# One program order from a list scheduler, and FFN gradients turned from SBUF to SBUF, in a transformer block's forward and backward pass

## The chip, the cores and the metric

The kernel runs on one core of one Trainium2 chip. The metric is the device time of one execution in microseconds (us). The engines of the core are TensorE (PE in the profile, with its weight loads as PEld), VectorE (DVE), ScalarE (ACT), GpSimd (POOL) and SyncE (SP, which here only issues DMAs). Each engine works through its own instructions in order, and semaphores hold it until what it needs is there.

## The reference

Inputs are bf16: x is 2048 x 512, the attention has 32 heads of 16, the FFN has 1792 hidden units. The forward pass is

```
h  = x + A(layernorm(x))        # A: q, k, v = x @ wqkv; each position attends to
                                # itself and 7 earlier ones, 2 apart; then @ wo
h2 = h + B(layernorm(h))        # B: gelu(x @ w1 + b1) @ w2 + b2, gelu in the tanh form
```

The kernel returns h2 and, for a given gradient of h2, the gradients of x, wqkv, wo, w1, b1, w2 and b2. So it computes the forward pass, the backward pass through FFN, attention and both layernorms, and four large weight gradients, each a sum over all 2048 positions.

## The kernel before

The 2048 positions are cut into 4 chunks of 512 (`c`), each of 4 tiles of 128 rows. The work has three stages.

**Attention forward** (`p1_*`). For each chunk: layernorm (L192), turning by PE transposes (`to_fm`), q, k and v (L351), dots of q with 8 shifted copies of k (L258: one DVE multiplication of 128 x 4096, summed by PE), softmax, products of the coefficients with rows of v that are gathered from DRAM by an indirect DMA from POOL (L250; products L288, two per tile of 128 x 2048; PE sums them, L293), the output projection (L446), and a second layernorm.

**FFN, forward and backward** (`p2_h`, `p2_rest`). PE computes the hidden layer (L520); ACT evicts it twice, as x (L522) and as its square (L523); ten steps on blocks of 4 hidden tiles give the gelu and its derivative: 9 on DVE (L528 to L537) and a tanh on ACT (L530). PE then multiplies by w2 (L555; the bias b2 and the residual h are added by two more matmuls, L556 and L557), computes the gradient of the hidden layer (L568, multiplied by the derivative on DVE at L571) and takes it back through w1 (L581). The gelu (`g_d`) and the gradient (`gh_d`) are stored to DRAM as they lie, hidden units on partitions (L538, L574).

**Attention backward and weight gradients** (from L601). DVE carries the dots (L882) and the products with gathered rows (L787); PE sums them (L888, L795) and computes the gradients of q, k, v (L822, L850). The order here is written out by hand: `slot` advances delayed steps and gives PE a quota of weight-gradient matmuls, which the generator `wgrads` hands out one by one (L643). A weight gradient needs its operands with positions on partitions, so `load_t` (L636) loads g and gh back from DRAM with a transposing DMA, 256 hidden units at a time (1 MiB), into two buffers `gwm`. Loads of the q, k, v gradients (L697) and the rows of the first layernorm (L692, 32 small DMAs) come behind gates at the end.

Plain DMAs go out on SP or POOL; the indirect ones on POOL only. Stores of weight gradients (L629), of h2 (L560) and of the gradient of x (L856) are on POOL. Buffers are pools that are released between the stages (L496, L604). The key lines:

```
638  SY.dma_start_transpose(out=t_[:], in_=src)     # load_t: DRAM to SBUF, turned
655  tiles.append(load_t(g_d[n * 256:(n + 1) * 256, :] if n < 7 else gh_d[...]))
692  SY.dma_start(out=r16[32 * j:32 * j + 32, 2 * sc:2 * sc + 2, :], in_=ap)
754  filler(dve_us * RATIO - pe)                     # PE's quota of weight gradients
```

Of the kernel before, what the change touches and what calls it, by code (L numbers as in the profile page):

```python
# [1 line left out]

# [8 lines left out]
P = 128  # L11
# [13 lines left out]
NEG = -30000.0  # L25

# [5 lines left out]
def _sub(apobj, dims, off=0):  # L32
    return _ap(apobj, [apobj.ap[0]] + [list(d) for d in dims], off)


@with_exitstack
def kernel(
# [36 lines left out]
    FB = [(0, 4), (4, 8), (8, 12), (12, 14)]  # L74

    def pool(name, bufs=1, side="left", space=None):
        kw = dict(name=name, bufs=bufs, side=side)
        if space is not None:
            kw = dict(name=name, bufs=bufs, space=space)
        if space is not bass.MemoryType.DRAM:  # L80
            kw["reuse_waits"] = "tile"
        return tc.alloc_tile_pool(**kw)

    pools = []

    def LP(name, side="left"):
        p = pool(name, 1, side)
        pools.append(p)
        return p

    const = LP("const")
    dram = pool("dram", 1, space=bass.MemoryType.DRAM)
    psY = pool("psY", 2, space=bass.MemoryType.PSUM)
    psT = pool("psT", 2, space=bass.MemoryType.PSUM)
    psX = pool("psX", 2, space=bass.MemoryType.PSUM)

    def X(name):
        return psX.tile([P, 2, 512], F32, name=name, tag="x")

    def Y(name):  # L100
        return psY.tile([P, 512], F32, name=name, tag="y")

    def TT(name):
        return psT.tile([P, 1024], BF16, name=name, tag="t")


    ident = const.tile([P, P], BF16, name="ident")
    make_identity(nc, ident[:])
    Pmat = const.tile([P, P], BF16, name="Pmat")
    V.tensor_copy(out=_sub(Pmat[:], [[1, 8], [8, DH]]), in_=_sub(ident[:], [[DH, 8], [1, DH]]))  # L110
    S32 = const.tile([P, 32], BF16, name="S32")
    for j in range(4):
        V.tensor_copy(out=S32[32 * j:32 * j + 32, :], in_=ident[32 * j:32 * j + 32, 32 * j:32 * j + 32])
    Sum4 = const.tile([P, P], BF16, name="Sum4")
    V.tensor_copy(out=Sum4[:].rearrange("p (a b) -> p a b", a=4), in_=S32[:].unsqueeze(1).to_broadcast([P, 4, 32]))
    nSum4 = const.tile([P, P], BF16, name="nSum4")
    V.tensor_scalar(out=nSum4[:], in0=Sum4[:], scalar1=-1.0, scalar2=None, op0=ALU.mult)
    Sm = const.tile([P, 4, P], BF16, name="Sm")
# [10 lines left out]
    mk = const.tile([16, 2, 4, 32], BF16, name="mk")  # L129
# [52 lines left out]

    def to_fm(src, dst):
        for hh in range(2):
            pt = TT("pt")
            for d2 in range(2):
                dc = 2 * hh + d2
                for j in range(TPC):
                    T.transpose(pt[:, d2 * 512 + j * P:d2 * 512 + (j + 1) * P], src[:, j, dc * P:(dc + 1) * P], ident[:])
            A.copy(out=dst[:, 2 * hh:2 * hh + 2, :], in_=pt[:].rearrange("p (a n) -> p a n", a=2))  # L190

    def layernorm(wp, src, rstd_all, c, dst):  # L192
        mv = wp.tile([P, TPC, 2], F32, name="mv", tag="mv", bufs=2)
        for j in range(TPC):
# [830 lines left out]
```

## Time and profile before

| | us |
|---|---|
| timed runs | 896.83, 905.11, 908.13 (median 905.11) |
| profiled execution: span from first to last instruction | 887.3 |
| PE busy, matmuls | 665.3 (75% of the span) |
| DVE busy | 530.4 (60%) |
| ACT busy | 339.6 (38%) |
| POOL busy | 175.3 (20%) |

The profile has no time of the profiled execution outside its span; the timed runs are 9.5 to 20.8 us longer than that span (the median 17.8 us). A busy share is a mean over stages with different limits, so the windows of the trace by stage are read first: 0 to 154 us is attention forward, 154 to 234 the passage to the FFN, 234 to 432 the FFN, 432 to 740 attention backward with weight gradients beside it, 740 to the end weight gradients alone. The granted TensorE clock is given as a share of full speed.

### The profile page before, as it was taken

The page shows a single profiled execution, that of the slowest core. Times are in us where ns is not written, and L with a number is a line of the kernel's source. Part 1 is how long each engine was busy: PE and PEld are TensorE (multiplying, and loading weights), DVE is VectorE, ACT ScalarE, POOL GpSimd, SP SyncE. Part 2 cuts the span into 40 slices and gives each one's busy share as a digit, 9 for nine tenths or more (in the row PEclk, how much of TensorE's full clock was granted, in tenths as well). Part 3 has the DMA queues.
Part 4 walks back from the last instruction along what each step waited for, and adds up shares of the span by engine and source line. Part 5 has one row for each costly group of instructions (what it writes and reads, how often), then busy time and mean ns, then how long its engine had stood idle before and what let it go on. Part 6 is the DMA issues. An engine that isn't in the chain of part 4 may idle for free.

```text
span 887.3 us, 10335 instructions
## 1 busy us (share of the span) xinstructions
PE 665.3 (75%) x3948; PEld 302.2 (34%) x3948; DVE 530.4 (60%) x774; ACT 339.6 (38%) x529; POOL 175.3 (20%) x221
## 2 busy tenths in 40 slices
PE   4888886467889899899853779791777688864486
PEld 2434432222334333334321324240222356731132
DVE  6799696368768687694657967972494852000000
ACT  2657674366445356340430533440233331100011
POOL 3304342200100001000006431240143222210011
PEclk9999997778999999999965789896787898977699
DMA  9637276841232233233994587899589654632343
GB/s 304 201 142 261 90 236 223 183 127 62 71 119 91 88 96 106 72 118 120 281 264 148 195 261 237 243 273 83 74 256 346 217 160 113 149 110 77 137 146 116
DMA packets 151280, 146.30 MB, mean 165 GB/s; under 512 B 94669, under 2 KB 139518, under 8 KB 146366
## 3 DMA queue, kind: packets, MB, share of 16 engines
q1 hardware_dynamic: 137102, 74.83, 33.5%
q0 software_dynamic: 14128, 70.81, 23.2%
q8 instruction: 31, 0.51, 0.2%
q14 instruction: 19, 0.16, 0.1%
HBM read 72.95 MB, written 48.03 MB: 136 GB/s over the span
## 4 chain that ended last, share of the span: by engine, by line
issue 30%; PE 13%; DVE 11%; DMA 7%; POOL 6%; ACT 3%; SPq 0%; POOLq 0%; DVEq 0%; ACTq 0%
DMA R<-q_d,rowi 4%; POOL out_dram L629 3%; PE ps_f L555 3%; DVE prb L787 2%; DMA R<-go_d,rowi 2%; PE ps_gg L568 2%; PE ps_gw L651 2%; PE ps_gl L581 2%; PE ps_h L520 1%; POOL R L250 1%; PE ps_go L822 1%; POOL out_dram L856 1%; DVE junk L219 1%; DVE gt L532 1%; ACT xb L522 1%
## 5 line engine op out<-in xcount | busy, mean ns | idle before, releaser
L787 DVE TENSOR_TENSOR prb<-R,cf 128x2048 bf16<-128x2048 bf16 x96 | 110.4, 1217 | 22.6 <-DMA R<-q_d,rowi 14.6
L520 PE MATMUL ps_h<-ln2T,w 128*128 128x512 bf16 x224 | 63.4, 411 | 23.3 <-ACT x L523 20.7
L651 PE MATMUL ps_gw<-gout_r,gwm 128*128 128x512 bf16 x224 | 61.0, 413 | 25.0 <-DMA gwm<-g_d 25.0
L795 PE MATMUL ps_band<-prb,S 128*32 128x512 bf16 x384 | 41.4, 466 | 44.6 <-DVE prb L787 43.7
L709 PE MATMUL ps_gwq<-gqh,ln_r 128*128 128x512 bf16 x192 | 44.0, 390 | 30.7 <-DMA gqh<-gq_d 25.9
L568 PE MATMUL ps_gg<-goT,w2T 128*128 128x512 bf16 x224 | 54.5, 378 | 11.0 <-DVE gb1p L571 8.6
L672 PE MATMUL ps_gw<-gwm,ln_r 128*128 128x256 bf16 x448 | 55.4, 282 | 8.3 <-ACT gwst L628 8.2
L629 POOL DMA_DIRECT2D out_dram<-gwst x58 | 31.4, 542 | 148.0 <-ACT gwst L628 107.3
L211 ACT ACTIVATE gyr<-ps_gl,rstd 128x512 bf16<-128x512 f32 x32 | 21.9, 686 | 99.0 <-PE ps_gl L850 65.3
L522 ACT ACTIVATE xb<-ps_h,b1c 128x512 bf16<-128x512 f32 x56 | 38.2, 686 | 45.0 <-PE ps_h L520 44.8
L555 PE MATMUL ps_f<-w,gt 128*128 128x512 bf16 x224 | 54.1, 384 | 1.0 <-DVE gt L532 1.0
L560 POOL DMA_DIRECT2D out_dram<-h2s x16 | 9.4, 591 | 227.9 <-ACT h2s L559 227.9
L351 PE MATMUL ps_qkv<-ln1T,wqkv 128*128 128x512 bf16 x192 | 49.3, 397 | 6.4 <-ACT kt L353 2.1
L672 PEld LDWEIGHTS <-ln_r 128*128 128x128 bf16 x448 | 44.5, 101 | 19.2 <-issue 12.5
L850 PE MATMUL ps_gl<-wqkvT,gqkvT 128*128 128x512 bf16 x192 | 46.1, 398 | 0.0
L219 DVE CUSTOM_DVE_ANT_0 junk<-gyr,ln1r 128x512 bf16<-128x512 bf16 x16 | 11.1, 691 | 56.7 <-ACT gyr L211 56.7
L520 PEld LDWEIGHTS <-w 128*128 128x128 bf16 x224 | 23.0, 103 | 57.7 <-issue 40.2
L797 ACT ACTIVATE gks<-ps_band 128x512 bf16<-128x512 f32 x32 | 19.0, 601 | 61.4 <-PE ps_band L795 55.1
L288 DVE TENSOR_TENSOR prb<-R,cf 128x2048 bf16<-128x2048 bf16 x32 | 37.4, 1211 | 8.1 <-PE ps_band L293 4.4
L651 PEld LDWEIGHTS <-gwm 128*128 128x128 bf16 x224 | 20.9, 103 | 61.2 <-DMA gwm<-g_d 25.5
L628 ACT ACTIVATE gwst<-ps_gw 128x256 bf16<-128x256 f32 (+1 forms) x42 | 19.1, 456 | 57.5 <-DMA out_dram<-gwst 36.7
L523 ACT ACTIVATE x<-ps_h,b1c 128x512 bf16<-128x512 f32 x56 | 38.1, 686 | 7.5 <-DMA ln_d<-ln 5.9
(325 smaller groups left out, 1228.6 us busy)
## 6 DMA issues: line engine op xcount, KB each, us to landing
g_d<-gt SPq DMA_DIRECT2D x12, 512.0 KB
ln_d<-ln POOLq DMA_DIRECT2D x8, 512.0 KB
out_dram<-gwst POOLq DMA_DIRECT2D x30, 128.0 KB
w<-in_B_w_dram POOLq DMA_DIRECT2D x2, 1792.0 KB
vw<-vf_d SPq DMA_DIRECT2D x4, 528.0 KB
xt<-in_A_x_dram SPq DMA_DIRECT2D x4, 512.0 KB
vf_d<-vt POOLq DMA_DIRECT2D x4, 512.0 KB
v_d<-tmst SPq DMA_DIRECT2D x8, 256.0 KB
```

The costliest lines, as they stand in the source:

```text
L351: T.matmul(ps[:, gg, :], lhsT=wqkv[:, dc, sel * D + g * P:sel * D + (g + 1) * P], rhs=st_[c]["ln1T"][:, dc, :], start=(dc == 0), stop=(dc ...
L520: T.matmul(ps[:, i, :], lhsT=w1[:, dc, f * P:(f + 1) * P], rhs=ln2T[c][:, dc, :], start=(dc == 0), stop=(dc == DC - 1))
L522: A.activation(out=xb[:, f - f0, :], in_=ps[:, i, :], func=ACT.Identity, bias=b1c[:, f:f + 1])
L555: T.matmul(ps[:], lhsT=gts[f // 4][:, f % 4, j * P:(j + 1) * P], rhs=w2[:, f, :], start=(f == 0), stop=False)
L568: T.matmul(ps[:, i, :], lhsT=w2T[:, dc, f * P:(f + 1) * P], rhs=goT[:, dc, :], start=(dc == 0), stop=(dc == DC - 1))
L629: G.dma_start(out=dst, in_=st[:, 0:width])
L651: T.matmul(ps[:], lhsT=gtm[:, t, (f % 2) * P:(f % 2 + 1) * P], rhs=r16[:, t, :], start=(t == 0), stop=(t == NT - 1))
L672: T.matmul(ps[:, 0:256], lhsT=r16[:, t, dc * P:(dc + 1) * P], rhs=ghm[:, t, :], start=(t == 0), stop=(t == NT - 1))
L709: T.matmul(pss[dd][:], lhsT=r16[:, i * HN + t, dc * P:(dc + 1) * P], rhs=hv[i][:, t, :], start=(i == 0 and t == 0), stop=(i == 1 and t == ...
L787: V.tensor_tensor(out=pr[:, hf].rearrange("p j (d h) -> p j d h", h=H), in0=R[:, o:o + 4, :].rearrange("p j (d h) -> p j d h", h=H), in1=c ...
L795: T.matmul(ps[32 * j:32 * j + 32, :], lhsT=S32[:], rhs=pr[:, hf, j, :], start=(hf == 0), stop=(hf == 1), skip_group_check=True)
L850: T.matmul(ps[:], lhsT=gqkv[c][:, b, j * P:(j + 1) * P], rhs=wqkvT[:, b, :], start=(b == 0), stop=(b == 11))
```

## The change

The whole program is now recorded as operations (`op`), each with an engine, a price in us, a function that issues its instructions, and the buffers it reads and writes. `schedule` ranks each operation by the longest priced path to the end (less a bias per chunk), then plays the program through on its prices: whenever an engine is free it takes the ready operation of highest rank whose buffers find a home in SBUF or PSUM. `emit` issues the operations in that order. There are no pools and no stages any more.

What is computed differs in these points. The gelu comes from ACT (L825), and with it 2 of the 9 DVE steps per block go; the square is taken from SBUF by ACT in one instruction per block (L821). 28 of the 32 layernorm scalings move from DVE to ACT (L519). Each pair of band products is one DVE instruction of 128 x 4096 (L602). b2 and h are added on DVE (L795, L855) and the two matmuls for them go; the gradient of b2 is summed by ACT (L868) in place of 16 matmuls. g and gh are turned from SBUF to SBUF right where they are made (`to_rows`, 32 transposing DMAs of 512 or 256 KB), stored to DRAM in rows, and loaded back by plain DMAs (`wload`). The gradient of w1 is summed in tiles of 512 or 256 columns in place of 256. The last chunk's q, k, v gradients stay in SBUF (`gs3`). Stores of h2, of weight gradients, of the gradient of x, and of both layernorms move from POOL to SP: SP issues 339 rows in place of 202, POOL 109 in place of 223.

The core of the diff (the original replaces nearly every line of the body):

```diff
+class Plan:
...
+    def schedule(self, log=None):
+        ops = self.ops
+        for o in reversed(ops):
+            own = o.us + (DMA_LAT + o.dma if o.dma is not None else 0.0) + SYNC
+            o.rank = own + max((ops[s].rank for s in o.succs), default=0.0)
+        for o in ops:
+            o.prio = -(o.rank - o.chunk)
...
+            for e in self.ENG:
+                if busy[e] > now + 1e-9 or not ready[e]:
+                    continue
+                later, pick = [], None
+                while ready[e]:
+                    it = heapq.heappop(ready[e])
+                    o = ops[it[1]]
+                    if alloc(o, now):
+                        pick = o
+                        break
+                    later.append(it)
...
+    def xload(dst, ap, src_ap, kb, r=(), key=None, tag="xload", after=()):
+        return op("SP", 0.4 + kb / 256.0, lambda: SY.dma_start_transpose(out=ap(), in_=src_ap()), r=r, w=[(dst, key)], dma=kb / XPOSE_RATE, tag=tag, after=after)
...
+        op("DVE", tt_us(4096), prod, r=[R, cf], w=[pr], tag="prod" + tag)
...
+            op("ACT", act_us(N), lambda xb=xb, x2=x2: A.activation(out=fl(x2), in_=fl(xb), func=ACT.Square), r=[xb], w=[x2], tag="x2")
...
+            op("ACT", act_us(N), lambda xb=xb: A.activation(out=fl(xb), in_=fl(xb), func=ACT.Gelu_apprx_tanh), w=[xb], tag="gelu")
+            op("ACT", act_us(N), lambda th=th: A.activation(out=fl(th), in_=fl(th), func=ACT.Tanh, scale=GC), w=[th], tag="tanh")
...
+            to_rows(xb, g_d[b], c, n, "g")
...
+    def to_rows(src, dst, c, n, tag):
+
+        tr = sb("xr" + tag, [P, 4 * n, P], tag="xr", lim=3)
+        xload(tr, lambda: tr(), lambda: src().rearrange("p a n -> p (a n)"), n * 128, r=[src], tag="xr" + tag)
+        store(dst, lambda: dst()[:, c, 0:4 * n, :], tr, lambda: tr(), n * 128, key=c, tag="rst" + tag)
...
+            op("DVE", tt_us(512, True), lambda j=j, ps=ps, h2s=h2s: V.tensor_tensor(out=h2s(), in0=ps(), in1=h_[c]()[:, j, :], op=ALU.add),
...
+    def wg_group(parts, rds, N, dst, tag):
+
+        ps = ps_("wg" + tag, 1, tag="wg", lim=3)
+        k = len(parts)
+        st = sb("wgs" + tag, [P, N], tag="wgs", lim=4)
+        for i in range(0, k, 4):
...
+            op("PE", 4 * MM * max(N, 280) / 512, mm, r=rds, w=[ps], tag="wg" + tag, al=[st])
...
+            wload(G_, lambda G_=G_, n=n: G_(), g_t[b][:, :, 0:4 * n, :], 512 * n, [g_d[b]], None, "gwin")
...
+    pl.schedule(LOG)
+    pl.emit()
...
-    def load_t(src):
-        t_ = gwp.tile([P, NT, 256], BF16, name="gwm", tag="gwm", bufs=2)
-        SY.dma_start_transpose(out=t_[:], in_=src)
-        return t_
...
-    def slot(dve_us):
...
-        filler(dve_us * RATIO - pe)
```

Two places show how the order moves. First SP, the queue of plain and transposing DMAs. Before, in attention backward, `gwm` is a 1 MiB piece of g or gh that is turned on its way from DRAM (`R` and `sh` are operands of attention backward):

```order
L638 DMA_TRANSPOSE gwm<-g_d 128x16x256 x2
L178 DMA ln1r<-ln_d 128x4x512
L835 DMA sh<-glf 32x2x512 x4
L638 DMA_TRANSPOSE gwm<-gh_d 128x16x256
L835 DMA sh<-attn 32x2x512 x4
L633 DMA ln_r<-ln_d 128x16x512
```

Now, in the FFN, on the same engine (`xb` holds a block of the gelu, `xrg` the same turned, `h2s` rows of the output):

```order
L489 DMA_TRANSPOSE xrg_1806<-xb_1695 128x16x128
L489 DMA_TRANSPOSE xrg_1840<-xb_1790 128x8x128
L485 DMA g_d_128<-xrg_1806 128x2048
L485 DMA g_d_129<-xrg_1840 128x1024
L489 DMA_TRANSPOSE xrg_1913<-xb_1818 128x16x128
L485 DMA out_dram<-h2s_1842 128x512
L485 DMA g_d_126<-xrg_1913 128x2048
```

The transposing DMAs have moved from attention backward into the FFN, each with a store behind it that needs its result, and the stores of the output stand between them.

Second PE, at the end. Before, behind the last matmuls of the gradient of x (L850), only weight gradients follow (`gwm` with L672 for w1, `o_r` with L685 for wo, `gqh` with L709 for wqkv):

```order
L850 MATMUL ps_gl_6061<-wqkvT,gqkvT 128x512
L672 MATMUL ps_gw_5965<-gwm,ln_r 128x256
L672 MATMUL ps_gw_6500<-gwm,ln_r 128x256
L685 MATMUL ps_gwo<-gh_2363,o_r 128x512
L685 MATMUL ps_gwo<-gh_3530,o_r 128x512
L709 MATMUL ps_gwq<-gqh,ln_r 128x512
```

Now the last weight gradients (L1003) stand between sums of band products (L611) and the gradient of x (L984):

```order
L984 MATMUL ps<-wqkvT_3471,gqkvT_4601 128x512
L1003 MATMUL ps<-gq3in_5253,rl_516_4968 128x512
L611 MATMUL ps<-prbk_5402,S 32x512
L1003 MATMUL ps<-gqs_5244,rl_543_5159 128x512
L626 MATMUL ps<-ident,gks_5408 128x128
L1003 MATMUL ps<-gq3in_5430,rl_516_4968 128x512
L1003 MATMUL ps<-gks_5545,rl_543_5159 128x512
L984 MATMUL ps<-wqkvT_3471,gqkvT_5278 128x512
```

What comes last on PE is the gradient of x of two chunks, not the weight gradients.

## Rows read from the trace of the kernel before

**Rows 1.** Windows by stage: length, busy PE, PEld, DVE, ACT, POOL, clock, DMA, GB/s.

```profile
0.00:154.00 154.00, 115.29 (x906) 54.31 (x906) 124.16 (x200) 91.39 (x113) 49.42 (x71) 0.96 0.61 207
154.00:234.00 80.00, 52.87 (x219) 20.31 (x218) 50.10 (x65) 46.00 (x65) 8.69 (x14) 0.80 0.48 122
234.00:432.00 198.00, 179.88 (x792) 74.75 (x792) 144.56 (x286) 82.03 (x139) 6.95 (x13) 1.00 0.35 104
432.00:594.00 162.00, 119.70 (x808) 48.99 (x808) 125.68 (x112) 62.24 (x96) 54.88 (x43) 0.80 0.79 241
594.00:638.00 44.00, 19.01 (x96) 6.82 (x95) 12.21 (x18) 3.61 (x11) 2.17 (x4) 0.69 0.98 97
638.00:740.00 102.00, 81.98 (x580) 41.17 (x578) 73.73 (x94) 37.50 (x73) 32.67 (x39) 0.88 0.70 221
740.00:887.30 147.30, 96.58 (x555) 55.86 (x552) 0.00 (x0) 16.86 (x36) 20.52 (x39) 0.84 0.42 124
```

**Rows 2.** Waits by line: engine, tile and line, releaser; us in total, times, longest.

```profile
PE ps_gw L651 <- DMA gwm<-g_d: 25.0, 1, 25.0
PE ps_gwq L709 <- DMA gqh<-gq_d: 25.9, 1, 25.9
```

**Rows 3.** SP in the timeline: start us, us, the two transposing DMAs.

```profile
586.10 41.71 SPq L638 DMA_TRANSPOSE gwm<-g_d  x2
```

**Rows 4.** DMAs by tile: ns on SP, min/median/max, first and last start.

```profile
L638 SPq DMA_TRANSPOSE gwm<-g_d x7: 4519/7646/23816, 444.2 to 604.0; - x7
L638 SPq DMA_TRANSPOSE gwm<-gh_d x7: 4202/4459/14755, 656.2 to 766.8; - x7
L547 SPq DMA_TRANSPOSE goT<-in_grad_out_dram x4: 1897/1949/2759, 192.2 to 381.5; - x4
L835 SPq DMA_DIRECT2D sh<-attn x16: 585/595/737, 462.0 to 663.1; - x16
```

**Rows 5.** Groups of DVE and ACT work: busy us, mean ns; idle before.

```profile
L205 DVE TENSOR_SCALAR ln<-xt,rstd,nm 128x512 bf16<-128x512 bf16 x16 | 5.8, 421 | 1.7 <-PE ps_qkv L351 1.7
L787 DVE TENSOR_TENSOR prb<-R,cf 128x2048 bf16<-128x2048 bf16 x96 | 110.4, 1217 | 22.6 <-DMA R<-q_d,rowi 14.6 <-DMA R<-go_d,rowi 5.8 <-PE ps_gw L672 0.9
L882 DVE TENSOR_TENSOR pr<-got,vw 128x4096 bf16<-128x4096 bf16 x16 | 36.0, 2286 | 2.6 <-DMA vw<-vf_d 2.1 <-issue 0.5
L534 DVE TENSOR_TENSOR x<-x,gt 128x2048 bf16<-128x2048 bf16 (+1 forms) x16 | 17.4, 1089 | 0.3
L390 DVE TENSOR_TENSOR m<-asb,ps_L 128x512 bf16<-128x512 bf16 x4 | 2.7, 668 | 0.0
L523 ACT ACTIVATE x<-ps_h,b1c 128x512 bf16<-128x512 f32 x56 | 38.1, 686 | 7.5 <-DMA ln_d<-ln 5.9 <-DVE dt__2659 L537 0.4 <-DVE dt__3090 L537 0.4
L530 ACT ACTIVATE a__1985<-a__1985 128x2048 bf16<-128x2048 bf16 x1 | 1.9, 1912 | 3.6 <-DVE a__1985 L529 3.6
```

**Rows 6.** PE prices: a piece of the chain (start, us), a timeline row, a group.

```profile
282.15 3.02 PE ps_f L555 x14
587.53 0.62 PE L795 MATMUL ps_band<-prb,S 128*32 128x512 bf16 x8
592.41 0.61 PE L305 MATMUL ptu<-ident,gks 128*128 128x128 bf16 x8
L557 PE MATMUL ps_f<-h,ident 128*128 128x512 bf16 x16 | 6.2, 390 | 0.0
```

**Rows 7.** Timeline of POOL and DVE, 459 to 486 us: start us, us.

```profile
459.55 9.13 DVE L787 TENSOR_TENSOR prb<-R,cf 128x2048 bf16<-128x2048 bf16 x8
465.89 12.41 POOL L250 DMA_INDIRECT R<-go_d,rowi  x1 [31.66 <-DMA sh<-attn]
468.60 8.89 DVE L882 TENSOR_TENSOR pr<-got,vw 128x4096 bf16<-128x4096 bf16 x4
481.07 0.96 POOL L250 DMA_INDIRECT R<-k_d,rowi  x1 [0.30 <-issue]
485.24 2.36 DVE L787 TENSOR_TENSOR prb<-R,cf 128x2048 bf16<-128x2048 bf16 x2 [5.83 <-DMA R<-go_d,rowi]
```

More of the change, by code (lines that the diff above doesn't have):

```diff
@@ L25 @@
 NEG = -30000.0
+BANK = 512
+NBANK = 8
+SYNC = 0.2
+DMA_LAT = 2.0
+DMA_RATE = 325.0
+XPOSE_RATE = 167.0
 def _ap(apobj, dims, off=0):
@@ L832, in shift, with recip, rmul @@
-    def shift(c, src):
-        sh = p3.tile([P, 2, 512], BF16, name="sh", tag="sh", bufs=2)
+        op("PE", 0.3, esum, r=[e], w=[pss], tag="sume")
+        def recip():
+            with nc.allow_low_precision(reason="bf16 softmax"):
+                V.reciprocal(out=r(), in_=pss()[:, 0:P])
+        op("DVE", 0.96, recip, r=[pss], w=[r], tag="recip")
+        psr = ps_("psr", 1)
+        def rmul():
+            for j in range(4):
+                T.matmul(psr()[:, j * P:(j + 1) * P], lhsT=Sm[:, j, :], rhs=r(), start=True, stop=True)
@@ new lines @@
+    N1 = [["DVE"] * 4, ["ACT"] * 4, ["ACT"] * 4, ["ACT"] * 4]
+    N2 = [["ACT"] * 4] * 4
+    p1_load(0)
+    for i in (1, 0, 2):
+        load(wqkv, lambda i=i: wqkv()[:, :, i * D:(i + 1) * D], lambda i=i: A_wqkv[:, i * D:(i + 1) * D].rearrange("(a p) j -> p a j", p=P), 512, key=i, tag="wqkv")
+    for c in range(1, NC):
+        pl.bias = P1_BIAS * c - 400.0
+        p1_load(c)
+    pl.bias = 0.0
+    for d_b, r in ((v_d[0], 0), (k_d[0], 0), (q_d[NC - 1], CH), (go_d[NC - 1], CH)):
+        op("SP", 0.4, lambda d_b=d_b, r=r: SY.dma_start(out=d_b()[r:r + RPAD, :], in_=zrow[:]), w=[(d_b, "b")], dma=0.1, tag="z")
@@ new lines @@
+    op("PE", 0.1, lambda: T.transpose(pb.bf()[:, 0:FT], b1b[:], ident[0:FT, 0:FT]), r=[B1B], w=[pb], tag="b1t")
+    op("DVE", 0.2, lambda: V.tensor_copy(out=b1c[:], in_=pb.bf()[:, 0:FT]), r=[pb], w=[B1C], tag="b1c")
+    for c in range(NC):
+        pl.bias = P1_BIAS * c - 400.0
+        p1_ln(c)
+        p1_qkv(c)
+        p1_attn(c)
+        p1_o(c)
+        pl.bias += H_BIAS
+        p1_h(c)
+    pl.bias = 0.0
+    load(w1, lambda: w1(), lambda: B_w1.rearrange("(a p) f -> p a f", p=P), 1792, tag="w1", after=[(attn, 1)])
@@ new lines @@
+    op("DVE", 0.1, lambda: V.memset(glf()[:, :, S:SP], 0.0), w=[(glf, "z")], tag="z", after=[(gh_[2], 0)])
+    for c in range(NC):
+        pl.bias = P3_BIAS * c
+        p3_go(c)
+        p3_dots(c)
+        if c:
+            p3_bands(c - 1, "v")
+        p3_bands(c, "q")
+        if c:
+            p3_bands(c - 1, "k")
+            p3_gl1(c - 1)
+    p3_bands(NC - 1, "v")
+    p3_bands(NC - 1, "k")
+    p3_gl1(NC - 1)
+    pl.bias = 0.0
+    wg_ffn()
+    gb = sb("gb", [P, FT + DC], F32)
+    gbb = sb("gbb", [P, FT + DC])
```

1564 lines of the change are left out of this document (801 added, 763 removed).

## The prediction

> **What bounds the kernel now.** I read the windows by stage first, since the page's means mix stages with different limits [rows 1]. In attention forward, 0 to 154 us, DVE is busy 124.16 of 154 (81%) at a clock near full: DVE paces it. From 154 to 234 us no engine is above 66%: the stage runs out of attention work before it is full of FFN work. The FFN, 234 to 432 us, is PE's: 179.88 of 198 us (91%) at full clock. After 432 us nothing is full for long. PE is busy 119.70 of 162 us at a clock of 0.80, then 19.01 of 44, then 81.98 of 102, and from 740 us on, with DVE at zero, 96.58 of 147.3 us at 0.84.
>
> Next the waits. The hole at 594 to 638 us is one wait of PE, 25.0 us, for `gwm`, a piece of g that is turned on its way from DRAM; another of 25.9 us stands at the end, for the q gradients [rows 2]. The first has its cause on SP: two transposing DMAs of 1 MiB took 41.71 us there [rows 3], where the shortest took 4.2 us and the usual ones 4.5 to 7.6 us [rows 4]. PE works in order, so the matmuls that DVE needs stood behind the weight gradient that had no operand, and DVE stopped too. So before this change the last 455.3 us (432 to 887.3) are set by waits, and the first 432 by DVE and PE work.
>
> **The change, stage by stage.** The sum is made against the span of the profiled execution, 887.3 us; the timed median lies 17.8 us above it.
>
> *Attention forward, 154 us.* On DVE 28 layernorm scalings of 0.42 us go to ACT (-11.8); 32 products of 1.22 us become 16 of 2.29 us, the price of the dots of the same size (-2.4); four additions of b2 come, priced as the product of their shape, 1.22 us (+4.9) [rows 5]. Net -9.3 us, at DVE's share of 0.81 -11.5 us. ACT gains 28 x 0.686 = 19.2 us [rows 5] on 91.39 [rows 1], 75% of the stage, below DVE. The start gets later: SP now issues the x of chunks 1 to 3 ahead of chunk 0's and of wqkv, 1.5 MiB more in front; at this stage's 207 GB/s [rows 1] that is 7.6 us if nothing covers it, nothing if the normalizing of the other chunks does. I take 5. Stage: 148 us.
>
> *Passage to the FFN, 80 us.* Its 219 matmuls cost 219 x (179.88 / 792) = 50 us at the FFN's price, 55 us at the FFN's share [rows 1]. That is the lower bound, if the order fills it; 80 is the upper. The new order, too, puts the last bands of attention forward nearly back to back, so I do not take the bound: 62 us.
>
> *FFN, 198 us.* The matmuls for b2 and h go: two groups of 6.2 us [rows 6], three quarters of them in this window, -9.3 us; at PE's share of 0.91 -10 us. DVE loses two of nine steps per block (two groups of 17.4 us) and gains 16 additions from PSUM at 0.67 us [rows 5]: three quarters of -24 is -18, from 144.56 to 127 us, off the path. ACT changes 56 squares of 0.686 us for 16 block-wide ones and gains as many gelus, both priced as the tanh, 1.91 us for a full block [rows 5] and about half that for the four short ones, plus 16 sums for b2 of some 0.7 us: about +20 us here on 82, half the stage. Both stay below PE, so they cost nothing; if PE were faster, DVE would be next. One table load more on ACT is one instruction. Stage: 188 us.
>
> The 32 transposing DMAs and their stores now lie here. DRAM to SBUF the rows say 1.9 us for 512 KB and 4.2 us for 1 MiB on SP at best, 41.71 / 2 = 20.9 us per MiB at worst [rows 3, 4]. No row has SBUF as the source; a gain or a loss against DRAM is open. I take 4.2 us per MiB, because the rows of `goT`, which stand in this same stage with no gathers beside them, are the nearest. The 14 MiB then cost SP 59 us of 250 (62 + 188), with 25 us for the 6 MiB of the other transposes and up to 36 us for 60 plain DMAs at 0.6 [rows 4]: hidden. The stores of h2, weight gradients and gx, now on SP, are some 90 of 0.4 to 0.6 us over all stages. On POOL they are gone.
>
> [...]
>
> *Everything after 432 us, 455.3 us.* PE's work at full clock: 704 matmuls of 512 columns for weight gradients (those of w1 counted as such), 192 for gx, 64 for the gradient of the attention output, 16 row sums, together 976 x (3.02 / 14) = 210.5 us; 512 sums of products at 0.62 / 8 = 39.7 us; 320 turnings at 0.61 / 8 = 24.4 us [rows 6]. Sum 274.6 us. DVE has 211.6 us there [rows 1] less 96 x 1.217 - 48 x 2.286 = 7.1 us [rows 5]: 204.5. If the weight gradients lie beside the bands, as the order has it, the stage is PE's, and I give PE the share it has in the FFN: 274.6 / 0.91 = 302 us; behind the last matmul come an eviction, five short DVE steps and a store, some 6 us. Stage: 308 us. DVE would be at 66%, less than the 78% it held from 432 to 594 us. [...]
>
> Sum: 148 + 62 + 188 + 308 = 706 us of span, 724 us with the 17.8 around it.
>
> **Rivals.** *Transposes from SBUF are dear* (the slow side). SP has 250 - 25 - 36 = 189 us for 14 MiB: from 13.5 us per MiB on SP sets the FFN, and from (189 + 181) / 14 = 26.4 the kernel is slower than before. At the slowest row, 20.9, it is 292 us, +103, so 827 us (0.05). At twice that, 41.7, it is 584 us, +395: 1119 us. For it: every stretch with two of them in flight and gathers beside them was slow. Against it: it needs a price that no row reaches. 0.10.
>
> *The gathers hold DVE.* A gather whose work on POOL took 0.96 us took 12.41 us while DVE ran products without a break, from 459.55 to 477.5 us, and ended when they ended; DVE then stood 5.83 us for its rows [rows 7]. In all DVE lost 20.4 us so (14.6 + 5.8) [rows 5], less than one such wait for each of 24 gathers. The new DVE instructions are longer, the gathers remain on POOL, and the planner's price for one does not know of it. If each of the 24 exposed 5.83 us: 204.5 / 0.78 + 140 = 403 us in place of 308, so 819 us. 0.15.
>
> [...]
>
> *The order does not hold.* The planner's prices are not the chip's; an engine in order then waits where the plan had none, as PE did for `gwm`. Then little more is won than the two great waits, 25.0 + 25.9 us: 905 - 51 = 854 us. 0.07. That even these are eaten, and nothing changes: 0.05.
>
> **Numbers.** The forecast, 724 us, has 0.58. Its own range goes from 658 us (all of PE's work, 115.3 + 50 + 170.6 + 274.6 = 610 us, packed at 95%, plus 6 and the smallest surplus, 9.5) to 795 us (attention forward at DVE 0.75, the passage unchanged, PE at 0.85 and 0.82 in the other two: 160 + 80 + 200 + 341, plus 14). The range that holds 8 in 10 reaches over the gathers (819), the moderate transposes (827) and the order that does not hold (854): 658 to 856. Outside lie no change, the slow side, and a little below. Two per cent is about what a measurement of this kernel tells from no change (its three runs span 1.2%): faster 0.58 + 0.15 + 0.05 + 0.07 = 0.85, the same 0.05, slower 0.10.
>
> **What would show it.** In the profile after: DVE's busy time near 495 us, ACT's near 390; PE at 85% or more of the span with a clock above 0.95; no wait of PE for an operand of a weight gradient above some 5 us; the end made of matmuls of gx and not of weight gradients; SP's transposes of 512 KB near 2 us each. The forecast is wrong if these take above 6 us on SP and PE waits in the FFN, if DVE waits for gathered rows again and again after the FFN, or if the passage around 150 us is still a hole.

## The result, and the profile after

The changed kernel took 711.13 us (median of 5 executions, 706.07 to 712.16), against a forecast of 724 and a range of 658 to 856. Its ratio to the kernel before is 0.797, interval 0.792 to 0.801. Measured again beside some of the experiments, it took 710.47 us (710.17 to 711.82, 6 executions), ratio 0.822 (0.818 to 0.827). The kernel before spreads far more than the changed one, from 859.78 to 907.77 us in 17 executions there, so the ratios, and the times of the experiments, leave out executions more than 1.5% above the fastest of their kernel.

The experiments are compared with the changed kernel's own 710.5 us. Of them, only the gate, the part alone in the kernel before and chunk 0's loads ran on the chip of that measurement; the others ran on three other chips. I go by times all the same, because the changed kernel moved by 0.1% between its two measurements while the fastest execution of the kernel before moved by 3%, from 887.05 to 859.78 us. A difference of 2 or 3% on another chip is therefore likely, but not shown: by ratio to the kernel before, the three that came out some 17 us slower (weight gradients ranked last, turning from DRAM, gelu on DVE) have 0.826, 0.831 and 0.832, with intervals that take in 0.822.

The profiled execution took 706.07 us around a span of 704.3. First the windows of that span, cut where its work changes: the last sums of attention forward end at 161 us, PE is full from 200 us, and the last matmul of the FFN begins at 401 us. The columns are those of [rows 1].

```profile
0.00:161.00 161.00, 121.11 (x934) 58.67 (x953) 127.22 (x171) 120.58 (x150) 48.08 (x60) 0.92 0.67 218
161.00:200.00 39.00, 26.34 (x123) 11.86 (x119) 22.48 (x34) 35.77 (x46) 3.17 (x5) 0.76 0.67 162
200.00:401.00 201.00, 192.83 (x934) 87.72 (x952) 146.92 (x291) 113.70 (x152) 3.64 (x3) 0.99 0.85 226
401.00:704.30 303.30, 266.14 (x1668) 118.66 (x1687) 193.57 (x180) 102.78 (x184) 50.87 (x39) 0.93 0.69 234
```

Against [rows 1]: the FFN's full stretch begins at 200 us and no longer at 234; it lasts 201 us, before 198; and what follows takes 303.3 us in place of 455.3. So 34 us come from the entry, none from the FFN, and 152 us from the stage behind it. There PE's busy time fell from 317.28 to 266.14 us: the granted clock was 0.93 in place of 0.69 to 0.88, and matmuls of this stage that took some 16 us now lie before 401 us. The rest of the stage, in which PE was not busy, fell from 138 to 37 us. The page gives the whole span:

```profile
PE 606.4 (86%) x3652; PEld 276.9 (39%) x3708; DVE 490.2 (70%) x675; ACT 372.8 (53%) x529; POOL 105.8 (15%) x107
```

The waits by line, engine first, then tile, line and what was waited for (total, times, longest), answer to [rows 2]. Behind the FFN these are the waits of PE and DVE for a DMA that the view lists:

```profile
DVE cfk L591 <- DMA shk<-glf: 7.8, 1, 7.8
PE ps L1003 <- DMA gq3in<-gv_d: 3.2, 1, 3.2
PE ps L1003 <- DMA gw1in<-gh_d: 2.8, 2, 2.2
DVE prbk L602 <- DMA Rk<-q_d,rowi: 2.5, 2, 2.0
DVE prbv L602 <- DMA Rv<-go_d,rowi: 0.7, 1, 0.7
```

The two waits of 25 us are gone; no operand of a weight gradient is waited for longer than 3.2 us, and gathered rows cost DVE 3.2 us in all. The transposing DMAs by tile (ns on SP, min/median/max), which answer to [rows 4]:

```profile
L489 SPq DMA_TRANSPOSE xrg<-xb x16: 1232/1903/4490, 145.8 to 342.5; - x16
L489 SPq DMA_TRANSPOSE xrh<-th x16: 1232/2274/7456, 219.4 to 397.2; - x16
L489 SPq DMA_TRANSPOSE goT<-in_grad_out_dram x4: 2414/2550/2642, 173.0 to 326.7; - x4
```

From SBUF they hold SP about as long as from DRAM: by the medians 1.9 and 2.3 us for blocks of 512 or 256 KB, against 2.6 us here and 1.9 us before [rows 4] for the 512 KB of `goT`. And four rows of the chain of what ended last (start, us):

```profile
683.67 0.86 PE ps L1003 x4
684.53 6.26 PE ps L984 x29
690.85 6.65 PE ps L984 x30
697.52 0.79 ACT gyr L640 x2
```

The last weight gradient (L1003) ends with the gradient of x (L984) behind it, as the order had it.

### The profile page after: what moved, and what is told of

The parts are those of the page before. It is cut to its first block, busy times and chain, and to the rows that moved or that the text cites. A ratio compares the mean times of both kernels' runs of the same rounds, so it can differ in the third digit from the quotient of the medians.

```text
span 704.3 us, 9741 instructions
## 1 busy us (share of the span) xinstructions
PE 606.4 (86%) x3652; PEld 276.9 (39%) x3708; DVE 490.2 (70%) x675; ACT 372.8 (53%) x529; POOL 105.8 (15%) x107
## 3 DMA queue, kind: packets, MB, share of 16 engines
q1 hardware_dynamic: 151120, 108.54, 53.1%
## 5 line engine op out<-in xcount | busy, mean ns | idle before, releaser
L1003 PEld LDWEIGHTS <-rl 128*128 128x128 bf16 x448 | 44.4, 101 | 57.2 <-issue 13.9
L816 PE MATMUL ps<-ln2T,w 128*128 128x512 bf16 x217 | 56.9, 404 | 11.2 <-ACT xb L818 7.5
L877 PE MATMUL ps<-goT,w2T 128*128 128x512 bf16 x222 | 54.6, 384 | 4.0 <-DVE th L879 3.8
L1003 PE MATMUL ps<-gw1in,rl 128*128 128x512 bf16 (+1 forms) x256 | 54.1, 373 | 2.8 <-DMA gw1in<-gh_d 2.8
L602 DVE TENSOR_TENSOR prbv<-Rv,cfv 128x4096 bf16<-128x4096 bf16 x16 | 36.2, 2286 | 28.9 <-PE ps L583 15.0
L890 PE MATMUL ps<-w1T,th 128*128 128x512 bf16 x217 | 52.8, 384 | 0.7 <-ACT gyr L640 0.4
L853 PE MATMUL ps<-w,xb 128*128 128x512 bf16 x217 | 52.6, 379 | 0.3
L1003 PE MATMUL ps<-rgo,gw2in 128*128 128x512 bf16 x219 | 50.5, 380 | 0.4 <-issue 0.2
L602 DVE TENSOR_TENSOR prbq<-Rq,cfq 128x4096 bf16<-128x4096 bf16 x16 | 35.9, 2286 | 21.3 <-PE ps L611 6.8
L693 PE MATMUL ps<-ln1T,wqkv 128*128 128x512 bf16 x183 | 45.8, 388 | 0.6 <-issue 0.2
L984 PE MATMUL ps<-wqkvT,gqkvT 128*128 128x512 bf16 x185 | 45.3, 391 | 0.8 <-issue 0.6
L879 DVE SCALAR_TENSOR_TENSOR th<-th,ps 128x512 bf16<-128x512 bf16 x56 | 37.3, 684 | 9.0 <-PE ps L877 8.9
L602 DVE TENSOR_TENSOR prbk<-Rk,cfk 128x4096 bf16<-128x4096 bf16 x16 | 35.7, 2286 | 5.8 <-PE ps L611 3.3
L602 DVE TENSOR_TENSOR prbo<-Ro,cfo 128x4096 bf16<-128x4096 bf16 x16 | 35.7, 2280 | 0.5 <-PE ps L583 0.5
```

What stands on the lines that cost most here:

```text
L602: V.tensor_tensor(out=pr().rearrange("p a j (d h) -> p a j d h", h=H), in0=_sub(R()[:, o0, 0:1], [[st, 2], [512, 4], [32, DH], [1, H]]), i ...
L693: T.matmul(ps()[:, gg * 512:(gg + 1) * 512], lhsT=wqkv()[:, dc, sel * D + g * P:sel * D + (g + 1) * P], rhs=st_[c]["ln1T"]()[:, dc, :], st ...
L816: T.matmul(ps(), lhsT=w1()[:, dc, f * P:(f + 1) * P], rhs=ln2T[c]()[:, dc, :], start=(dc == 0), stop=(dc == DC - 1))
L853: T.matmul(ps(), lhsT=d["g"][f // 4]()[:, f % 4, j * P:(j + 1) * P], rhs=w2()[:, f, :], start=(f == 0), stop=(f == FT - 1))
L877: T.matmul(ps(), lhsT=w2T()[:, dc, f * P:(f + 1) * P], rhs=goT()[:, dc, :], start=(dc == 0), stop=(dc == DC - 1))
L879: op("DVE", 0.79, lambda f=f, ps=ps, z=z, f0=f0: V.scalar_tensor_tensor(out=z()[:, f - f0, :], in0=z()[:, f - f0, :], scalar=1.0, in1=ps() ...
```

## The experiments

Where nothing else is said, a kernel is the changed one with the edit shown. The scheduler plans every kernel anew, so an edit can move work that it doesn't name.

**The changed kernel once more**, as the yardstick beside other runs.

> The changed kernel itself once more, unedited, as the yardstick beside the next three on the same chip: 711 us within 1.5%, ratio to the kernel before 0.79 to 0.81.

Measured: 710.47 us. The time is as expected; the ratio to the kernel before is 0.822, above the 0.79 to 0.81, because the kernel before was faster beside it, as told above.

**Weight gradients ranked last.**

```diff
-    pl.bias = 0.0
+    pl.bias = 10000.0
     wg_ffn()
```

> All as in the changed kernel, but every weight-gradient operation is ranked behind everything else, so that the scheduler puts them after attention backward. Theory A (the gain is the order: weight gradients beside the band products): the 704 weight-gradient matmuls (152 us at 0.216 us each) lose most of their cover, and attention backward becomes paced by DVE (about 194 us busy behind the FFN, at 0.78 to 0.85 of the stretch some 230 to 250 us). Time 401 + 240 + 140, about 780 us, between 760 and 800. Rival B (the gain is the turning from SBUF, which took the 25 us wait and the half clock away): the place of the weight gradients matters little, under 735 us.

Measured: 728.07 us (724.10 to 734.13). My expectation was wrong, since the edit does not take the cover away: a list scheduler gives a free PE whatever is ready, however low its rank. The windows of this kernel from 570 us:

```profile
570.00:640.00 70.00, 70.00 (x469) 30.37 (x462) 52.55 (x76) 32.62 (x69) 10.56 (x7) 1.00 0.59 208
640.00:725.00 85.00, 65.07 (x321) 31.30 (x318) 0.00 (x0) 11.43 (x21) 0.00 (x0) 0.93 0.41 129
```

Only the last 85 us, with DVE at zero, are weight gradients alone (147.3 us before the change [rows 1]). Beside the 710.5 us, the rank of this work is worth some 17 us (on another chip). What its place is worth needed another edit.

**Weight gradients gated.**

```diff
-    go = r16("rgo", lambda c: [...], [(st_[NC - 1]["d"][2], None)])
+    go = r16("rgo", lambda c: [...], [(SX, None)])
```

> All as in the changed kernel, but the first load of the weight gradients waits for the last step of the gradient of x, so that none of the 704 matmuls can lie beside attention backward (ranking them last did not do that: they still filled PE's gaps). Theory A (the cover of weight gradients is worth what they take): attention backward alone takes DVE's 194 us at 0.8 to 0.85 of the stretch, 230 to 245 us from 401 us on, then 152 us of matmuls at 0.95 and some 10 us until the first rows are there: 795 to 820 us. Rival B (the order is worth little, the gain came from shorter work and from turning in SBUF): under 750 us.

Measured: 810.18 us (803.32 to 812.70), ratio to the kernel before 0.936 (0.926 to 0.946), beside the changed kernel's 0.822. Its windows: to the end of the FFN, attention backward, weight gradients.

```profile
0.00:373.00 373.00, 318.14 (x1876) 148.17 (x1877) 280.28 (x487) 265.18 (x343) 53.78 (x67) 0.93 0.75 209
373.00:605.00 232.00, 157.14 (x1100) 61.93 (x1097) 202.66 (x178) 82.49 (x138) 55.89 (x40) 0.72 0.64 202
605.00:807.30 202.30, 159.16 (x737) 73.41 (x736) 3.64 (x11) 27.09 (x49) 0.00 (x0) 0.91 0.47 164
```

Attention backward alone is DVE's (202.66 of 232 us, 87%), with PE at a clock of 0.72; then the weight gradients stand alone for 202 us. Theory A holds in its sum, though two of its terms were off: the FFN ended 28 us earlier than I had put it, and the weight gradients took 202 us, not 170. All of their cover is worth 810.2 - 710.5 = 100 us against none. That is not what the change added, for the kernel before had part of the cover: from 432 to 740 us its PE already did 80 of the 177 us of these matmuls. Its rows for that stretch, of L651 and of L672:

```profile
432.00:740.00 308.00, 60.97 (x224) 20.88 (x224) 0.81 0.79 214
432.00:740.00 308.00, 19.31 (x152) 14.45 (x153) 0.81 0.79 214
```

How much of the gain is the cover that was added, no run isolates. What is shown is that without any cover the rest of the change still leaves the kernel 6.4% faster than the one before.

**Turning on the way from DRAM.**

```diff
-        xload(tr, lambda: tr(), lambda: src().rearrange("p a n -> p (a n)"), ...)
-        store(dst, lambda: dst()[:, c, 0:4 * n, :], tr, ...)
+        store(dst, lambda: dst()[:, c * CH:(c + 1) * CH].rearrange("(a p) m -> p a m", p=P), src, ...)
...
+        for h in range(n // 2):
+            xload(G_, lambda h=h: G_()[:, h], lambda h=h: t[h * 256:(h + 1) * 256, :], 1024, ...)
```

> All as in the changed kernel, but the gelu and its gradient are stored as they lie and turned on the way back from DRAM, 1 MiB at a time, as before the change; the scheduler plans with a price for it. Theory A (the order hides the turning wherever it stands): within 2% of 711 us, 700 to 725, PE waits for these loads under 10 us in all. Rival B (turning from DRAM beside the gathers is slow, and the change gains by taking it away): at the 20.9 us per MiB that the two slow ones took before, 14 MiB are 292 us against the 184 us in which these weight gradients now run (386 to 570 us), so PE waits up to 100 us for them; 740 to 820 us.

Measured: 729.80 us (721.75 to 732.26, 3 of 5 executions), 11 to 22 us above the changed kernel, on another chip. Neither number was met: the price is far below that of rival B, and just above A's. The wait and the tile's row show where it is:

```profile
PE ps L1001 <- DMA gw1in<-gh_d: 11.6, 2, 10.3
```

```profile
L489 SPq DMA_TRANSPOSE gw1in<-gh_d x7: 4114/6340/18226, 483.8 to 573.4; - x7
```

One of these loads held SP for 18.2 us, near the 20.9 us of each of the slow two before [rows 3], but a planner that prices and places the loads leaves only 11.6 us of such waits, where the order written by hand left 25.0.

**That part alone, in the kernel before.**

```diff
+    def turn(src, dst, c, n):
+        tr = ff.tile([P, 16, P], BF16, name="xr", tag="xr", bufs=2)
+        SY.dma_start_transpose(out=tr[:, 0:4 * n, :], in_=src[:, 0:n, :].rearrange("p a n -> p (a n)"))
+        SY.dma_start(out=dst[:, c, 0:4 * n, :], in_=tr[:, 0:4 * n, :])
...
-        SY.dma_start_transpose(out=t_[:], in_=src)
+        SY.dma_start(out=t_[:], in_=src)
```

> The kernel before with this one part of the change: gelu and its gradient are turned from SBUF to SBUF in the FFN and stored in rows, and the weight gradients load them by plain DMAs; its order, written by hand, stays. Theory A (the order is the larger part): the 25.0 us wait goes and part of the low clock beside it, FFN unchanged since its DMA engines were busy only 0.35 of the time; 890 less 25 to 45 us, 845 to 870 us, ratio to before 0.95 to 0.975. Rival B (turning in SBUF is most of the gain): under 800 us. Rival C (no gain: what waits next takes its place): 880 us or more.

Measured: ratio 1.004 (0.998 to 1.009), no difference. Its profile, of its fastest execution (span 853.8 us), has no wait for `gwm` any more, but the end is weight gradients alone as before (windows), and the other wait stands (waits by line):

```profile
154.00:234.00 80.00, 57.86 (x232) 22.44 (x229) 53.47 (x73) 48.14 (x67) 8.71 (x14) 0.81 0.66 150
234.00:432.00 198.00, 176.38 (x778) 73.25 (x776) 141.38 (x280) 80.66 (x140) 7.91 (x13) 1.00 0.66 159
594.00:638.00 44.00, 38.94 (x252) 15.08 (x251) 38.84 (x45) 14.91 (x29) 14.59 (x15) 0.92 0.66 224
740.00:853.80 113.80, 70.04 (x352) 34.63 (x349) 0.00 (x0) 12.13 (x23) 12.44 (x23) 0.85 0.36 120
```

```profile
PE ps_gwq L716 <- DMA gqh<-gq_d: 25.8, 1, 25.8
```

So the hole of [rows 2, 3] can be closed by this part, and the ratio does not gain by it. Over all executions the medians are 888.06 and 868.28 us. Whether the five of the kernel before that are compared, 859.78 to 869.44 us, have the hole at all stays open: its only trace spans 887.3 us. The first two windows give a price as well: from 154 to 432 us the DMA share was 0.66, before the change 0.48 and 0.35 [rows 1], which makes some 75 us of all 16 engines for 14 MiB turned from SBUF, an estimate of 5.4 us per MiB. The FFN is no longer for it.

**Every block turned twice.**

```diff
+        t2 = sb("xs" + tag, [P, 4 * n, P], tag="xs", lim=2)
+        xload(t2, lambda: t2(), lambda: src().rearrange("p a n -> p (a n)"), n * 128, r=[src], ...)
```

> All as in the changed kernel, but each of the 32 transposing DMAs from SBUF to SBUF is issued a second time, into a scratch tile that nobody reads. SP issues take 1.2 to 7.5 us each there, about 70 us in all, and the 16 DMA engines are busy 0.84 of the 200 us of the FFN (0.35 before the change). Theory A (hidden with room to spare): within 2% of 711 us. Rival C (the DMA engines are now near their limit in the FFN): the rise from 0.35 to 0.84 is about 98 us of all engines, as much again makes 266 us of work for 200 us, and buffers of gelu and gradient come free late; 730 to 780 us, with PE waiting in the FFN.

Measured: 759.39 us; its three other executions took 771.03 to 779.10, and the trace is of the last. That is rival C's number, but not its place: PE hardly waits in the FFN, and the time is lost behind it. The windows from 200 to 500 us of the kernel with turning from DRAM, of the changed one, and of this one; the DMA share is the last column but one.

```profile
200.00:300.00 100.00, 97.49 (x446) 43.63 (x445) 74.49 (x150) 62.61 (x86) 0.00 (x0) 0.99 0.39 119
300.00:400.00 100.00, 97.49 (x511) 44.73 (x510) 72.17 (x147) 50.83 (x71) 3.00 (x3) 1.00 0.69 207
```

```profile
200.00:300.00 100.00, 95.04 (x428) 42.65 (x435) 76.43 (x156) 61.89 (x85) 0.00 (x0) 0.99 0.76 190
300.00:400.00 100.00, 96.84 (x503) 44.62 (x513) 70.50 (x136) 51.30 (x67) 3.64 (x3) 0.98 0.93 263
400.00:500.00 100.00, 92.28 (x613) 40.31 (x621) 80.15 (x68) 41.08 (x68) 18.48 (x16) 0.95 0.89 294
```

```profile
200.00:300.00 100.00, 94.62 (x428) 42.09 (x426) 77.38 (x161) 63.97 (x88) 0.00 (x0) 0.98 1.10 233
300.00:400.00 100.00, 92.83 (x470) 42.39 (x467) 62.41 (x131) 46.26 (x67) 2.23 (x2) 0.95 1.03 244
400.00:500.00 100.00, 40.97 (x280) 17.76 (x279) 42.88 (x30) 19.81 (x25) 6.75 (x6) 0.69 1.07 181
```

The first copy is hidden: PE has 97.49 us of 100 without it and 95.04 with it. With the second the DMA engines are full (shares of 1.03 to 1.10), and the stage behind the FFN waits: PE 34.5 us for `gw2in`, DVE 33.5 us for the shifted coefficients. SP comes near its end too: by the sum of its timeline it issues for 95 and 86 us of the two stretches of 100 from 200 us, in the changed kernel for up to 57 and 75. So this run does not tell the engines from SP. The queue of these DMAs gives a price; its row on the page (packets, MB, share of 16 engines), of the changed kernel and of this one:

```profile
q1 hardware_dynamic: 151120, 108.54, 53.1%
```

```profile
q1 hardware_dynamic: 209488, 123.23, 64.6%
```

From 53.1% of 704.3 us to 64.6% of 777.3 us is 128 us of all 16 engines for 14 MiB, or 9.1 us per MiB. This is a price among full engines, against the 5.4 above, and a rough one: the same queue with the same bytes has 60.3% of 705.3 us, 425 us and not 374, in the trace of the kernel with chunk 0's loads first (below).

**Gelu on DVE.** From the tanh, in two steps per block.

```diff
-            op("ACT", act_us(N), lambda xb=xb: A.activation(out=fl(xb), in_=fl(xb), func=ACT.Gelu_apprx_tanh), ...)
+            op("DVE", ts_us(N), lambda ub=ub, th=th: V.tensor_scalar(out=fl(ub), in0=fl(th), scalar1=0.5, scalar2=0.5, ...))
+            op("DVE", tt_us(N), lambda ub=ub, xb=xb: V.tensor_tensor(out=fl(xb), in0=fl(ub), in1=fl(xb), op=ALU.mult), ...)
```

> All as in the changed kernel, but the gelu is made on DVE from the tanh (two steps per block of 4 hidden tiles, priced by the rows before at 17.4 us per step over the kernel) in place of one ACT instruction per block (1.9 us each, about 27 us). Theory A (both engines have room in the FFN; PE is the bound there): within 1% of 711 us, 705 to 718. Rival D (ACT paces the entry to the FFN, 9.3 to 10 us of each 10 from 170 to 200 us): faster by 5 to 10 us, 700 to 706, with PE's gap before 200 us shorter. Rival E (DVE, 147 of 200 us in the FFN, becomes the bound with 35 us more): 720 to 735 us.

Measured: 726.21 and 729.57 us (the other two 738.77 and 741.08), 17 us more, on another chip: rival E's number, and its reason only in part. DVE is not full in the FFN, whose last matmul begins at 403.8 us:

```profile
200.00:400.00 200.00, 185.17 (x889) 82.91 (x888) 158.99 (x307) 90.48 (x133) 2.55 (x1) 0.97 0.79 199
L892 PE MATMUL ps<-w1T,th x224: 379/379/634, 231.9 to 403.8; 128*128 128x512 bf16 x112
```

At 159 of 200 us DVE has room, but PE waits for it longer: for the product that makes the gradient of the hidden layer (`th`) 13.5 us in place of 6.3. Yet the FFN ends only 3.8 us later than in the unedited kernel (400.0), and the larger part is lost behind it. Whether that part comes of the edit or of the new order, one run does not tell.

**Band products in halves.** The prices that the scheduler sees are the same, and so is its order.

```diff
-            V.tensor_tensor(out=pr().rearrange("p a j (d h) -> p a j d h", h=H), ...)
+            for a in range(2):
+                V.tensor_tensor(out=pr()[:, a].rearrange("p j (d h) -> p j d h", h=H), ...)
```

> All as in the changed kernel, in the same order, but each of the 64 band products of 128x4096 is again two DVE instructions of 128x2048. By the rows 2 x 1.217 us stand against 2.286 us, so DVE gets 64 x 0.148 = 9.5 us more work. Theory A (a gather seldom waits for DVE): 2 to 9 us slower than the 710.5 us of the unedited kernel, 712 to 720. Rival G (the long product holds the gathers back; DVE stood 7.5 to 12.8 us for gathered rows): the shorter instructions let them through, those waits go, 705 us or less.

Measured: 711.36 us (709.45 to 715.30), no difference. Fusing gained nothing that can be measured, and it cost nothing. Single gathers do depend on the product: four that took 2.11 to 2.78 us in the unedited kernel beside the experiments took 1.23 to 1.71. The one that cost time did not. In that unedited kernel it began at 605.79 us, while DVE did products without a break from 601.04 to 618.73, and ended 0.9 us behind the last of them; DVE then stood for rows (POOL and DVE, start, us):

```profile
605.79 13.80 POOL L565 DMA_INDIRECT Rk<-q_d,rowi  x1 [5.46 <-DVE prbq L602]
628.65 4.49 DVE L602 TENSOR_TENSOR prbk<-Rk,cfk 128x4096 bf16<-128x4096 bf16 x2 [9.92 <-DMA Rk<-q_d,rowi]
```

With the halves it took 14.21 us and DVE stood 9.57. So rival G's wait exists, but shorter products do not let this gather through.

**Chunk 0's loads first.**

```diff
+    pl.bias = -400.0
     p1_load(0)
```

> All as in the changed kernel, but chunk 0's x and wqkv get the same urgency as the x of chunks 1 to 3 (its loads stood behind theirs on SP: the first projection began at 21.5 us, at 14.5 us before the change). Theory A (the start is on the path, since DVE and PE are both busy over 75% until 130 us): faster by 4 to 8 us against the unedited kernel. Rival F (DVE's statistics of chunks 1 to 3, done meanwhile, only move): within 2 us of it.

Measured: 708.79 us (704.59 to 713.88, 4 of 6 executions; the others 719.04 and 725.10): no difference, but not for rival F's reason. Windows of this kernel, then of the unedited one beside it, of the first 20 us and from the end of the FFN on:

```profile
0.00:20.00 20.00, 10.34 (x44) 4.78 (x45) 15.57 (x58) 6.40 (x7) 4.30 (x19) 1.00 0.80 247
390.00:705.30 315.30, 272.87 (x1720) 121.29 (x1717) 193.49 (x177) 104.66 (x184) 48.89 (x40) 0.92 0.75 238
```

```profile
0.00:20.00 20.00, 2.37 (x17) 1.73 (x18) 15.38 (x60) 4.77 (x6) 5.50 (x20) 1.00 0.73 229
400.00:708.70 308.70, 269.35 (x1687) 118.43 (x1685) 193.55 (x180) 102.39 (x182) 59.07 (x39) 0.92 0.67 230
```

PE does 8 us more work in the first 20 us, and the FFN's last matmul begins 10 us earlier (390.1 against 400.0). The order planned behind it then takes 315.3 us in place of 308.7.

**ACT relieved at the entry to the FFN.**

```diff
-    N2 = [["ACT"] * 4] * 4
+    N2 = [["ACT"] * 4] * 3 + [["DVE"] * 4]
...
+            if c == 0:
+                op("DVE", tt_us(N), lambda xb=xb, x2=x2: V.tensor_tensor(out=fl(x2), in0=fl(xb), in1=fl(xb), ...))
...
-               r=[goT], w=[jk, (GB2, (dc, c))], tag="gb2")
+               r=[goT], w=[jk, (GB2, (dc, c))], tag="gb2", after=[(d["g"][3], None)])
```

> All as in the changed kernel, but ACT is relieved at the entry to the FFN, where it was busy 28.8 of 30 us (170 to 200 us): the second layernorm of chunk 3 goes to DVE (4 x 0.8 us), the squares of chunk 0 go to DVE (4 blocks, up to 1.9 us each on ACT, 1.2 on DVE), and the four sums for b2 of chunk 0 (4 x 0.8 us) wait until its last gelu. Theory A (ACT paces this stretch): 12 us of its work leave it, PE's 24 us of gaps between 130 and 200 us shrink by 5 to 10, 700 to 706 us. Rival H (the order of DVE and the gathers before 170 us sets the entry, ACT only follows): within 3 us of 710.5.

Measured: 700.70 us (697.30 to 704.58, 5 executions; a sixth took 707.97), 1.4% faster, and as much below the 711.36 us that the halved products had on the same chip. The number is theory A's, the place is so only in part. Windows of the unedited kernel, then of this one:

```profile
170.00:200.00 30.00, 19.35 (x75) 8.45 (x75) 16.79 (x23) 27.90 (x37) 0.42 (x1) 0.72 0.81 187
570.00:640.00 70.00, 52.37 (x300) 21.77 (x299) 51.29 (x46) 19.28 (x35) 23.11 (x11) 0.78 0.83 286
```

```profile
170.00:200.00 30.00, 22.45 (x90) 9.94 (x91) 21.24 (x30) 24.75 (x31) 0.00 (x0) 0.77 0.75 175
570.00:640.00 70.00, 67.86 (x524) 32.03 (x523) 55.67 (x53) 32.97 (x62) 20.08 (x12) 1.00 0.86 284
```

At the entry PE gains 3 us; the FFN ends at 398.6 in place of 400.0 us. The rest is a hole at 570 to 640 us that the new order does not have. In the unedited kernel DVE waited there 9.9 us for the gathered rows shown under the halves and 8.8 us for shifted coefficients, here for no gathered rows and 3.9 us for shifted coefficients. So 1.4 of the 13 us between the two traces stand at the entry, and the rest where the edit changes nothing but the order. Part of it may also come and go by itself: in the first trace of the unedited kernel the gathered rows `Rk` cost 2.5 us, as shown above.

**Small loads on ACT's queue.**

```diff
+                if name == "rl1":
+                    op("ACT", 0.5, lambda c=c, ap=ap, src=src: A.dma_start(out=ap(bs[c]()), in_=src), r=rd, ...)
+                    continue
                 load(bs[c], ...)
```

> All as in the changed kernel, but the 32 small loads of the first layernorm's rows (64 KB each, 0.59 us of issue) go out on ACT's queue in place of SP's. On SP they stood for 15 us in front of the shifted coefficients of the last two chunks, and DVE waited 7.8 to 8.8 us for those, in a stretch (570 to 640 us) in which PE is busy 52 to 56 of 70 us. Theory A (SP's order is what holds them): that wait falls under 3 us, 702 to 708 us. Rival I (the DMA engines, 0.83 to 0.86 busy there, or ACT's own queue take as long): within 2 us of 710.5, or slower if ACT stands behind a load that has to wait for its buffer.

Measured: 716.64 us (714.67 to 719.75): slower, rival I's last case. DVE's wait for the shifted coefficients did fall, from 8.8 to 2.3 us, but ACT then stood behind the loads. From ACT's timeline (start, us; in brackets the idle time before):

```profile
569.60 16.55 ACTq L1016 DMA_DIRECT2D rl<-ln_d  x7
586.25 0.69 ACT L640 ACTIVATE gyr<-ps,rstd 128x512 bf16<-128x512 f32 x1 [16.20 <-DMA rl<-ln_d]
603.11 20.16 ACTq L1016 DMA_DIRECT2D rl<-ln_d  x24
623.31 0.58 ACT L494 CAST wgso<-ps 128x512 bf16<-128x512 f32 x1 [19.75 <-DMA rl<-ln_d]
```

**Both entries together**: the edits of the start and of ACT's relief.

> The two edits of the start and of the entry to the FFN together: chunk 0's x and wqkv first, and ACT relieved by chunk 3's second layernorm, chunk 0's squares and the delayed sums for b2. Alone the first ended the FFN 10 us earlier (390.1 against 400.0 us) and gave all of it back after 400 us, the second took 9 us off in all (701.6 us). Theory A (the two entries add up and what follows keeps the gain): FFN's end near 388 us, 690 to 698 us. Rival J (the order planned after 400 us is another one and gives it back, as for the first edit alone): FFN's end near 388 us all the same, but 700 to 712 us.

Measured: 691.86 us (690.05 to 694.05, 5 executions), ratio to the kernel before 0.794 (0.786 to 0.802): 2.6% below the changed kernel, on another chip, and the fastest of all. A sixth execution took 2767.73 us, and nothing on record tells why. The FFN's last matmul begins at 379.1 us:

```profile
L893 PE MATMUL ps<-w1T,th x224: 376/379/390, 216.6 to 379.1; 128*128 128x512 bf16 x112
```

That is 21 us earlier than in the unedited kernel (400.0) and 9 earlier than either theory had it; this time most of it is kept, 18.6 us in the time. Theory A's number, 690 to 698, is met.

## Why the prediction was right

- *The sum*, 706 us of span, met 704.3, and its parts nearly so: entry 148 + 62 = 210 against 200 us, FFN 188 against 201, the rest 308 against 303. The split of the entry was off (161 + 39), because the new order starts FFN work inside attention forward, from 97 us on. The FFN is 13 us longer than forecast, since the order lays work of the next stage into it (some 16 us of matmuls of L912, L583, L548 and L1003); PE is 96% busy there. That the sum comes out within 2 us is in part luck: +13, -10 and -5 offset each other.
- *The time around the span* was the term that failed. I added 17.8 us, the timed median less the span of one profiled execution. The changed kernel needed 1.8 (706.07 around 704.3), and every execution whose span is on record, of either kernel, 1.7 to 2.2. The profiled execution of the kernel before was simply a faster one than those timed. With 2 us the forecast would have been 708 against 711.13; the 13 us that it lies too high are this term.
- *The stage behind the FFN is PE's if the weight gradients lie beside the bands*: right. PE is busy 88% of it (0.91 forecast), and with the gate, which takes the cover away, DVE holds 87% and the kernel is 100 us slower. How much of the gain is cover that the kernel before did not have is not shown. DVE at 87% is above the 78% that I read from 432 to 594 us.
- *The transposing DMAs are hidden*: right, but I counted one resource alone. I summed SP's time and put the point of decision at 13.5 us per MiB there. SP's blocks took the 2 us that I had (medians of 1.9 and 2.3 us for 512 KB or less), but the DMA engines went from a share of 0.35 to 0.85 in the FFN, which my sum did not have. Turning twice filled them (shares of 1.03 to 1.10), with SP nearly full beside them. The engines' price, an estimate from the windows and the queue's rows above, was 5.4 us per MiB where they had room and 9.1 where they were full.
- *The gathers hold DVE*: the sum went by the rows, 20.4 us in 24 gathers; it was 3.2 us in the first trace and 12.8 in the second of the same kernel, most of it behind one gather of 13.80 us. Shorter products made four other gathers shorter, from 2.11 to 2.78 us down to 1.23 to 1.71, but not that one (14.21 us). The cost stayed far from the 140 us that 24 waits of 5.83 us would make.
- *The start*: I took 5 us. PE's first projection came 7 us later, and the experiment shows 10 us up to the end of the FFN, which the later order evens out.
- *What would show it*: DVE 490.2 (near 495), PE 86% (85% or more), no wait of a weight gradient above 3.2 us, the end of gx: met. ACT 372.8 (near 390) and the clock, 0.931 (above 0.95), were not. The one table load more on ACT took 1.28 us, at 142.60 us. One sign of being wrong came in part: the passage is still a hole, shorter by 34 us, with PE busy 45.7 of the 70 us from 130 to 200. Another gap lies from 530 to 640 us.
- One more step was only half right: I took the two waits of 25 us for the cause of the last 455 us. Closing the first alone moved the ratio by nothing.

## What to carry to other kernels

Look for the engine that is idle while another sets the pace, and for work that depends on neither: laying some 160 us of matmuls beside 200 us of vector work was worth 100 us against laying none there. When a step is moved to another place, count all that it uses there, the DMA engines as well as the queue that issues. With a planner in the kernel a local edit moves everything behind it, by some 10 us either way here: read where the time changed before naming the edit as its cause.

## What the runs showed of the hardware

Turning from SBUF to SBUF cost all 16 DMA engines an estimated 5.4 us per MiB in the kernel before with that part alone, where they were 0.66 busy, and 9.1 where every block was turned twice and they were full (1.03 to 1.10). In the changed kernel SP was held for 1.9 us by the median block of `xrg`, and for 1.2 to 7.5 us by all 32 blocks. A transposing DMA of 1 MiB from DRAM held SP for 4.2 to 23.8 us in the kernel before [rows 4], and for 4.1 to 18.2 us where the scheduler placed it (`gw1in`). Of 24 indirect DMAs from POOL behind the FFN in the second trace of the changed kernel, 23 took 0.9 to 2.9 us there; one took 13.80 us beside products that DVE did without a break, and ended 0.9 us behind the last. A DMA of 64 KB took 605 ns of issue on ACT's queue by the median of 32, and 595 ns on SP's (`sh`, [rows 4]); ACT did nothing else while 24 of them went out in 20.2 us.
